# Token-row loads of q, k and V by GpSimd from the fourth batch on, in a kernel of windowed attention and a two-layer MLP

## The chip, the core and the metric

The kernel runs on one core of a Trainium2 chip. Its engines are TensorE (PE; the profile shows its weight loads apart, as PEld), VectorE (DVE), ScalarE (ACT), GpSimd (POOL) and SyncE (SP); 16 DMA engines move data between memory and the core. The metric is the time of one execution in microseconds, the median over several runs.

## The reference

Eight batches of eight heads, 576 tokens, head dimension 64. Every token attends to itself and the 63 before it; the attention output, as 4608 rows of 512, goes through two matrix products with `h - tanh(h)` between them.

```python
scores = scale * np.matmul(q, k.transpose(0, 1, 3, 2))
mask = (rel >= 0) & (rel < window)          # window = 64
attn = softmax(np.where(mask, scores, -1e9))
x = np.matmul(attn, v).transpose(0, 2, 1, 3).reshape(4608, 512)
h = x @ w_in                                 # 512 x 2048
out = (h - np.tanh(h)) @ w_out               # 2048 x 512
```

Inputs and output are float32. The kernel computes in bfloat16 with float32 sums.

## The kernel before

**The MLP sets the beat.** Rows are cut into nine chunks of 512 tokens. A chunk has 16 steps: `hp_mm` (four matmuls of 512 columns, L304) makes one 128-row slice of h in a PSUM bank that alternates between two, ScalarE takes the tanh (L308), VectorE subtracts (`g_sub`, L314) into `gT`. Sixteen steps later `yp_mm` (four matmuls, L324) uses those slices for the output, ScalarE copies a finished tile (`y_out`, L329) and SyncE stores it. The program is a list of half-steps h: at even h stands `hp_mm` of step h/2, at odd h `yp_mm` of step h/2 - 16. Everything else is hung on a half-step by `at(h, function, ...)` and is issued there, after the MLP's matmul and before the subtraction. There is no scheduler: each engine does its instructions in just that order, and waits where data is not there.

**Attention works on pairs of heads.** A batch b has four pairs; pair pr takes heads pr and pr + 4, and g = 4b + pr counts pairs. For a pair, q and k are needed transposed (`qT`, `kT`: 128 rows are two heads of 64 columns); `scores` (L247) multiplies a span of 128 keys with 64 queries of both heads, nine times, and ScalarE takes the exponential; `masking` (L255) clears what is outside the window; `pv` (L261) multiplies with V and a column of ones; `norm` (L268, L272) divides. `x_dma` (L293) transposes the batch's result by DMA into the MLP's `xT`.

**V as key spans.** `vw` (two buffers, by the parity of the batch) holds for each of nine spans j its 128 keys as partitions: keys 64j to 64j+63 in partitions 64 to 127, the 64 keys before them in partitions 0 to 63, and per head 64 columns and a one.

**How batches 3 to 7 get their data.** The first three batches follow a script of steps (`PLAN`), which is the same in both kernels. From the fourth batch (b = 3) a loop places the work. With s = 32b - (0, 2, 4, 4, 4) and a = 8g - 48 - (the same), so that a = s - 48 for a batch's first pair and 8 more for each next one:

- V: one GpSimd DMA with cast to bfloat16 (`load_v_all`, L151, 72 partitions of 8 tokens) at s-78; a GpSimd copy per pair into `vb` (`cast_v`, s-72 on); nine SyncE DMAs that lay `vb` out as spans (`keys_v`, L161, from s-54), one that copies the upper halves into the lower (`shift_v`, L169, s-47).
- q and k: one GpSimd DMA each with cast (`load_all`, L101, 96 partitions of 6 tokens, so 1,536 contiguous bytes a row and head), k at s-64 and q at s-60. For b below 7: a GpSimd copy per pair into rows of two heads (`cast`, a-7 and a-5), six TensorE transposes of 96 rows (`tr`, L234, q at a, k at a+2), and the eviction of PSUM (ScalarE and VectorE for q, ScalarE for k), with a stride of six tokens.
- For b = 7, GpSimd copies instead into a zero-padded `qz` (`cast_q`, L120) and into rows of k; SyncE writes both to DRAM (`bounce`, L126 and L130) and reads them back transposed (`tr_dma`, L137 and L140).
- `pace` (L108) is a GpSimd copy of one element that waits for the subtraction of step h/2 - 1, so that a load does not start earlier.

For all of them, scores stand at a+5, a+7 and a+9, masking at a+11, `pv` at a+13 to a+15, `norm` at a+15.

Of the kernel before, what the change touches and what calls it, by code (L numbers as in the profile page):

```python
# [8 lines left out]
BF16 = mybir.dt.bfloat16  # L9
# [6 lines left out]
def kernel(  # L16
# [9 lines left out]
    nc = tc.nc  # L26
    B, H, S, D = q.shape
    NP = H // 2
    NJ = S // 64
    E, P = 6, S // 6  # L30
    EV, PV = 8, S // 8
    d_model = moe_w_in.shape[0]
    d_ff = moe_w_in.shape[1]
    NT = B * S
# [8 lines left out]
    const = ctx.enter_context(tc.tile_pool(name="const", bufs=1))  # L43
    qk_pool = ctx.enter_context(tc.tile_pool(name="qk", bufs=3))
    all_pool = ctx.enter_context(tc.tile_pool(name="all", bufs=2))
# [2 lines left out]
    sm_pool = ctx.enter_context(tc.tile_pool(name="sm", bufs=3))  # L48
    xt_pool = ctx.enter_context(tc.tile_pool(name="xt", bufs=3))
    g_pool = ctx.enter_context(tc.tile_pool(name="g", bufs=2))  # L50
    dram = ctx.enter_context(tc.tile_pool(name="dram", bufs=2, space=bass.MemoryType.DRAM))
    psum = ctx.enter_context(tc.tile_pool(name="psum", bufs=1, space=PSUM))


# [1 line left out]
    ps = psum.tile([128, 8, 512], F32, name="ps")  # L56

    ident = const.tile([128, 128], BF16, name="ident")
# [7 lines left out]
    NR, NPT = 2, 4  # L66
# [3 lines left out]
    vw = [const.tile([128, NJ, H, D + 1], BF16, name=f"vw{i}") for i in range(2)]  # L70
    vb = const.tile([PV, EV, H, D + 1], BF16, name="vb")
    PT = [const.tile([128, NJ, 128], BF16, name=f"pt{i}") for i in range(NPT)]
    kT = [const.tile([128, 64 + S], BF16, name=f"kt{i}") for i in range(NR)]
    qT = [const.tile([128, 2, S], BF16, name=f"qt{i}") for i in range(NR)]
    qz = [const.tile([P, 2, E, 128], BF16, name=f"qz{i}") for i in range(2)]
    xs = [const.tile([128, NJ, NP, D], BF16, name=f"xs{i}") for i in range(2)]

    stage, rows, whole = {}, {}, {}

    def move(eng, o, i):  # L80
        if eng is nc.scalar:
            nc.scalar.activation(o, i, ACT.Copy)  # L82
        else:
            eng.tensor_copy(o, i)  # L84

    def load(g, n, eng):

        b, pr = divmod(g, NP)
        if eng is nc.gpsimd:
            if (b, n) not in whole:  # L90
                whole[b, n] = all_pool.tile([P, H, E * D], BF16, tag=n, name=n + "all")
            t = whole[b, n][:, pr::NP]
        else:
            t = qk_pool.tile([P, 2, E * D], F32, tag="f", name=n + "f")
        eng.dma_start(out=t, in_=(q if n == "q" else k)[b, pr::NP].rearrange("h (p e) d -> p h (e d)", e=E))
        stage[g, n] = t

    def load_all(b, n):

        t = all_pool.tile([P, H, E * D], BF16, tag=n, name=n + "all")  # L100
        nc.gpsimd.dma_start(out=t, in_=(q if n == "q" else k)[b].rearrange("h (p e) d -> p h (e d)", e=E))  # L101
        for pr in range(NP):
            stage[b * NP + pr, n] = t[:, pr::NP]
# [6 lines left out]
    def cast(g, n, eng=nc.gpsimd):  # L110
# [1 line left out]
        move(eng, t.rearrange("p e h d -> p h e d"),  # L112
             stage.pop((g, n)).rearrange("p h (e d) -> p h e d", d=D))
        rows[g, n] = t

    def cast_q(g):

        i = stage.pop((g, "q")).rearrange("p h (e d) -> p h e d", d=D)
        for h in range(2):
            nc.gpsimd.tensor_copy(qz[g % 2][:, h, :, 64 * h:64 * h + 64], i[:, h])  # L120

    def bounce(g, n):

        if n == "q":
            t = dram.tile([2, S, 128], BF16, tag="q", name="qd")
            nc.sync.dma_start(out=t.rearrange("h (p e) c -> p h (e c)", e=E),  # L126
                              in_=qz[g % 2].rearrange("p h e c -> p h (e c)"))
        else:
            t = dram.tile([S, 128], BF16, tag="k", name="kd")
            nc.sync.dma_start(out=t.rearrange("(p e) c -> p (e c)", e=E),  # L130
                              in_=rows.pop((g, "k")).rearrange("p e h d -> p (e h d)"))
        rows[g, n + "d"] = t

    def tr_dma(g, n):
        t = rows.pop((g, n + "d"))
        if n == "q":
            nc.sync.dma_start(out=qT[g % NR].rearrange("c h s -> c (h s)"),  # L137
                              in_=t.rearrange("h s c -> (h s) c"), transpose=True)
        else:
            nc.sync.dma_start(out=kT[g % NR][:, 64:], in_=t, transpose=True)  # L140

    def load_v(b, pr):
        if (b, "v") not in whole:
# [20 lines left out]
    def shift_v(b, j0, j1, eng=nc.sync):  # L164
        lo, hi = vw[b % 2][0:64, j0 + 1:j1 + 1], vw[b % 2][64:128, j0:j1]
        if eng is nc.vector:
            eng.tensor_copy(lo, hi)
        else:
            eng.dma_start(out=lo.rearrange("p j h c -> p (j h c)"), in_=hi.rearrange("p j h c -> p (j h c)"))  # L169

    w_in_r = moe_w_in.rearrange("(ko ki) f -> ki ko f", ki=128)

# [23 lines left out]
    def more_constants():  # L196
# [7 lines left out]
        for h in range(2):  # L204
# [2 lines left out]
                                    base=-1, pattern=[[-1, 64]], channel_multiplier=1)  # L207
            nc.gpsimd.affine_select(hide[:, h], hide[:, h], compare_op=ALU.is_ge, fill=-(2.0 ** 30),
                                    base=64, pattern=[[1, 64]], channel_multiplier=-1)

    def more_zeros(i):
        nc.gpsimd.memset(qz[i], 0.0)

    def make_mask():
        nc.gpsimd.memset(seen, 1.0)
# [41 lines left out]
    def pv(g, grp):  # L257
        b, pr = divmod(g, NP)
        for i in range(3):
            j = 3 * grp + i  # L260
            nc.tensor.matmul(ps[:, 5 + grp, 130 * i:130 * i + 130], PT[g % NPT][:, j, :],  # L261
                             vw[b % 2][:, j, 2 * pr:2 * pr + 2, :], start=True, stop=True)

    def norm(g):
        b, pr = divmod(g, NP)
# [71 lines left out]
    def at(h, *fn):  # L337
        items.setdefault(h, []).append(fn)
# [14 lines left out]
    def play(script):  # L353
        for step in script.split():
            what = step[0]
            n = [int(i, 36) for i in step[1:] if i not in "apvs"]
            eng = [ENG[i] for i in step[1:] if i in "apvs"]
            if what in "qr":
                load(*n, "q" if what == "q" else "k", *eng)
            elif what in "QK":  # L360
                load_all(*n, what.lower())
# [12 lines left out]
            elif what == "z":  # L374
                for j in (0, 4) if eng[0] is nc.vector else (0,):
                    shift_v(*n, j, j + 4 if eng[0] is nc.vector else NJ - 1, *eng)
            elif what == "E":
                tr(*n, "q", 3, *eng)
            elif what == "F":
                tr(*n, "k", 2 if n[0] < 2 * NP else 3, *eng)  # L380
            elif what == "R":
                scores(*n, (4, 0, 1)[n[1]] if n[0] < NP else 4)
            elif what == "P":
                for i in range(3):
                    pv(*n, i)
                norm(*n)
            elif what == "M":
                masking(*n)
            elif what == "X":
                b, half, part = n  # L390
                x_tr(b, half, 4 * part, 4 + 5 * part, 2 if part == 1 and b < 2 else 3, *eng)
            elif what == "Y":
                x_dma(*n)
            elif what == "w":
                load_w_in(*n)
            elif what == "o":
                load_w_out(*n)
            elif what == "i":
                make_ident()
            elif what == "n":  # L400
                make_mask()
            elif what == "m":
                more_constants()
# [27 lines left out]
    for h, script in PLAN.items():  # L431
        at(h, play, script)

    for i in range(2):
        at(66 + 2 * i, more_zeros, i)


    for g in range(3 * NP, B * NP):
        b, pr = divmod(g, NP)
        a = 8 * g - 48 - (0, 2, 4)[min(b - 3, 2)]  # L440
        s = 32 * b - (0, 2, 4)[min(b - 3, 2)]
        at(s - 72 + 5 * pr, cast_v, b, pr)
        if b < 7:
            at(a - 7, cast, g, "q")
            at(a, tr, g, "q", 3, nc.scalar, nc.vector)
        else:
            at(a - 14, cast_q, g)
            at(a - 12, bounce, g, "q")
            at(a - 6, tr_dma, g, "q")
        if b < 7:  # L450
            at(a - 5, cast, g, "k")
            at(a + 2, tr, g, "k", 3, nc.scalar)
        else:
            at(a - 13, cast, g, "k")
            at(a - 11, bounce, g, "k")
            at(a - 5, tr_dma, g, "k")
        for i in range(3):
            at(a + 5 + 2 * i, scores, g, i, 4)
        at(a + 11, masking, g)
        for i in range(3):  # L460
            at(a + 13 + i, pv, g, i)
        at(a + 15, norm, g)
        if pr == NP - 1:
            at(a + 16, x_dma, b)
        for j in range(NJ):
            if pr == 0:
                at(s - 54 + j // 2, keys_v, b, j)
        if pr == 0:
            if b < 4:
                at(s - 78, load_v_all, b)  # L470
                at(s - 64, load_all, b, "q")
                at(s - 63, load_all, b, "k")
            else:
                hq, hk = s - (60 if b < 7 else 68), s - (64 if b < 7 else 72)
                for h, f in (s - 78, (load_v_all, b)), (hq, (load_all, b, "q")), (hk, (load_all, b, "k")):
                    at(h, pace, h)
                    at(h, *f)
            at(s - 47, shift_v, b, 0, NJ - 1)

    LAG = 16  # L480
    for h in range(min(items), 2 * (16 * NC + LAG) + 2):
        n = h // 2
        c, m = divmod(n, M)
# [41 lines left out]
```

## Time and profile before

Three runs took 353.01, 354.48 and 355.05 us, a median of 354.48. The profiled execution's span, from its first to its last instruction, is 351.4 us.

| Group (line, engine) | instructions | busy us | mean of one, ns |
|---|---|---|---|
| L304 PE, h | 576 | 147.7 | 380 |
| L324 PE, out | 576 | 146.1 | 381 |
| L247 PE, scores | 288 | 36.4 | 226 |
| L261 PE, PV | 288 | 29.6 | 226 |
| L234 PE, transposes of q and of k | 168 + 168 | 12.6 + 12.2 | 214, 210 |
| L314 DVE, subtraction | 144 | 99.3 | 691 |
| L272 DVE, norm | 64 | 48.3 | 755 |
| L308 ACT, tanh | 144 | 85.9 | 597 |
| L84 POOL, copies of V, k, q | 29 + 26 + 24 | 30.6 + 21.7 + 20.0 | 1069, 837, 832 |
| L167 DVE, lower half of `vw`, in the first batches | 4 | 3.3 | 854 |

How to read it: an instruction's duration is from its start to its end, and matmuls overlap, so four L304 matmuls of 380 ns advance the chain by 0.86 us. A group's line gives busy time and mean, then the idle time of its engine just before it and what ended most of it. The chain of waits follows what ended last back through the execution; each piece is start, length, engine or DMA, what it writes, line. The slices cut the span in 40 equal parts (8.8 us each) and give the busy share in tenths. In the DMA view a packet's size is what it writes; a queue's share is the time that its packets took as a share of 16 engines' time, and goes over 100% where packets of one engine overlap.

### The profile page before, as it was taken

What the parts mean: (1) busy time and instruction counts of PE and PEld (TensorE: products, weight loads), DVE (VectorE), ACT (ScalarE), POOL (GpSimd) and SP (SyncE); (2) the same over time, 40 slices, a digit from 0 to 9 for tenths busy, and PEclk for the clock granted to TensorE, in tenths of its full rate; (3) what the DMA queues carried; (4) which work ended last, traced back from release to release, by engine and by line L of the source; (5) the groups of instructions that cost most, each with busy time, mean ns of one, the idle gap of its engine ahead of it and who ended that gap; (6) DMA issues with size and microseconds to landing.
All of it is one profiled execution on the core that took longest, in us unless ns stands there. A gap on an engine that the chain in (4) does not pass through costs nothing.

```text
span 351.4 us, 5740 instructions
## 1 busy us (share of the span) xinstructions
PE 315.1 (90%) x2173; PEld 179.0 (51%) x2173; DVE 199.0 (57%) x314; ACT 192.8 (55%) x347; POOL 112.0 (32%) x160
## 2 busy tenths in 40 slices
PE   0267788899899999999999999997999999999995
PEld 0256366555555555555555555553555444444442
DVE  1336786867676666666776766663656333344400
ACT  1467479765556665666566666652554444444411
POOL 7829543833338325422642264410000000000000
PEclk9988999999999999999999999998999999999999
DMA  8699999969777696958494895669711400010021
GB/s 175 126 164 190 175 189 173 183 133 180 161 148 112 127 137 146 139 126 156 102 160 105 164 169 123 130 147 206 189 46 38 121 32 30 31 60 30 30 89 62
DMA packets 54436, 43.98 MB, mean 125 GB/s; under 512 B 25144, under 2 KB 48248, under 8 KB 54024
## 3 DMA queue, kind: packets, MB, share of 16 engines
q0 software_dynamic: 20512, 18.22, 35.8%
q1 hardware_dynamic: 33128, 24.37, 27.0%
q10 hardware_dynamic: 768, 1.02, 1.0%
q8 instruction: 17, 0.28, 0.3%
q14 instruction: 11, 0.09, 0.1%
HBM read 36.70 MB, written 11.21 MB: 136 GB/s over the span
## 4 chain that ended last, share of the span: by engine, by line
PE 78%; DVE 7%; DMA 5%; ACT 5%; POOL 2%; issue 2%; SPq 0%; ACTq 0%; DVEq 0%; POOLq 0%
PE ps L324 34%; PE ps L304 32%; PE ps L261 5%; PE ps L247 4%; DVE xs L272 3%; PE ps L234 3%; DMA vw<-vb 3%; DMA vall<-in_v_dram 2%; DVE gT L314 2%; ACT th L308 1%; DVE qt L84 1%; ACT pt L251 1%; ACT qt L82 1%; DMA kt<-kd 1%; DVE pt L255 1%
## 5 line engine op out<-in xcount | busy, mean ns | idle before, releaser
L314 DVE TENSOR_TENSOR gT<-ps,th 128x512 bf16<-128x512 f32 x144 | 99.3, 691 | 94.9 <-ACT th L308 92.6
L304 PE MATMUL ps<-xT,wi 128*128 128x512 bf16 x576 | 147.7, 380 | 1.7 <-DVE gT L314 1.7
L324 PE MATMUL ps<-w_out_sb,gT 128*128 128x512 bf16 x576 | 146.1, 381 | 0.2 <-ACT ysb L329 0.2
L308 ACT ACTIVATE th<-ps 128x512 f32<-128x512 f32 x144 | 85.9, 597 | 79.8 <-PE ps L304 79.5
L304 PEld LDWEIGHTS <-wi 128*128 128x128 bf16 x576 | 61.4, 114 | 47.7 <-issue 3.6
L324 PEld LDWEIGHTS <-gT 128*128 128x128 bf16 x576 | 54.3, 98 | 55.9 <-issue 1.0
L251 ACT ACTIVATE pt<-ps 128x384 bf16<-128x384 f32 x96 | 46.9, 490 | 44.9 <-PE ps L247 38.3
L272 DVE TENSOR_TENSOR xs<-ps,rc 64x576 bf16<-64x576 f32 x64 | 48.3, 755 | 1.5
L84 POOL COPY vb<-vall 72x1024 bf16<-72x1024 bf16 x29 | 30.6, 1069 | 52.8 <-DMA vall<-in_v_dram 40.2
L247 PE MATMUL ps<-qt,kt 128*128 128x128 bf16 x288 | 36.4, 226 | 8.5 <-ACT pt L251 3.8
L261 PEld LDWEIGHTS <-pt 128*128 128x128 bf16 x288 | 22.7, 101 | 19.8 <-issue 3.6
L261 PE MATMUL ps<-vw,pt 128*128 128x130 bf16 x288 | 29.6, 226 | 3.4 <-DVE xs L272 1.1
L247 PEld LDWEIGHTS <-kt 128*128 128x128 bf16 x288 | 24.4, 102 | 12.1 <-DMA kt<-kd 2.1
L329 ACT ACTIVATE ysb<-ps 128x512 f32<-128x512 f32 x36 | 21.5, 597 | 16.0 <-PE ps L324 16.0
L84 DVE COPY qt<-ps 64x576 bf16<-64x576 bf16 x24 | 18.2, 759 | 18.1 <-ACT qt L82 18.1
L84 POOL COPY kb<-kall 96x768 bf16<-96x768 bf16 x26 | 21.7, 837 | 13.0 <-DMA kall<-in_k_dram 12.1
L84 POOL COPY qb<-qall 96x768 bf16<-96x768 bf16 x24 | 20.0, 832 | 16.8 <-DMA qall<-in_q_dram 16.8
L82 ACT ACTIVATE qt<-ps 64x576 bf16<-64x576 bf16 x32 | 20.3, 636 | 1.0 <-PE ps L234 0.6
L82 ACT ACTIVATE kt<-ps 128x576 bf16<-128x576 bf16 x25 | 16.2, 648 | 4.3 <-PE ps L234 4.0
L255 DVE TENSOR_TENSOR pt<-pt,ps 128x1152 bf16<-128x1152 bf16 x24 | 17.9, 745 | 0.0
L234 PE MATMUL ps<-ident,kb 96*128 96x96 bf16 x168 | 12.2, 210 | 2.7 <-ACT xT L82 0.9
L234 PEld LDWEIGHTS <-kb 96*128 96x128 bf16 x168 | 10.2, 100 | 7.4 <-issue 2.7
(52 smaller groups left out, 123.4 us busy)
## 6 DMA issues: line engine op xcount, KB each, us to landing
out_dram<-ysb SPq DMA_DIRECT2D x36, 256.0 KB
vall<-in_v_dram POOLq DMA_DIRECT2D x7, 576.0 KB, 10.0
kall<-in_k_dram POOLq DMA_DIRECT2D x7, 576.0 KB, 8.8
qall<-in_q_dram POOLq DMA_DIRECT2D x7, 576.0 KB, 8.8
vw<-vb SPq DMA_DIRECT2D x61, 65.0 KB
vw<-vw SPq DMA_DIRECT2D x6, 520.0 KB
w_out_sb<-in_moe_w_out_dram POOLq DMA_DIRECT2D x4, 512.0 KB, 8.4
qd<-qz SPq DMA_DIRECT2D x4, 288.0 KB
```

The lines of the kernel that those rows point to most:

```text
L82: nc.scalar.activation(o, i, ACT.Copy)
L84: eng.tensor_copy(o, i)
L234: nc.tensor.transpose(tp[:, e, :], src[:, e, :], ident[:P, :P])
L247: nc.tensor.matmul(sp[:, i, :], kT[g % NR][:, 64 * j:64 * j + 128], qT[g % NR][:, :, 64 * j:64 * j + 64], start=True, stop=g >= 2 * NP)
L251: nc.scalar.activation(PT[g % NPT][:, 3 * grp:3 * grp + 3, :], sp, ACT.Exp, scale=scale)
L261: nc.tensor.matmul(ps[:, 5 + grp, 130 * i:130 * i + 130], PT[g % NPT][:, j, :], vw[b % 2][:, j, 2 * pr:2 * pr + 2, :], start=True, stop=True)
L272: nc.vector.tensor_tensor(xo[r, :, :, pr, :], ov[r, :, :, h, 0:D], rc[r].to_broadcast([64, 3, 3, 64]), ALU.mult)
L304: nc.tensor.matmul(hp, w_in_tile(ki, m), chunk_tile(c)[:, :, ki % 2, 64 * (ki // 2):64 * (ki // 2) + 64], start=(ki == 0), stop=(ki == 3))
L308: nc.scalar.activation(th, hp, ACT.Tanh)
L314: nc.vector.tensor_tensor(gT[c][:, m, :], hp, th, ALU.subtract)
L324: nc.tensor.matmul(yp, gT[c][:, m, s * 128:(s + 1) * 128], w_out_sb[:, m, :], start=(m == 0), stop=(m == M - 1))
L329: nc.scalar.activation(ysb, ps[:, yp_bank(c, s), :], ACT.Copy)
```

## The change

For batches 3 to 7 all loads become token rows: a partition is a token, a row is one head's 64 values (256 bytes read, 128 written).

- V: five GpSimd DMAs (`load_rows`, half-steps s-59 to s-55) put blocks of 128 tokens straight into `vw`: block i fills both halves of span 2i+1, the last one (64 tokens) the upper half of span 8. Heads stand in their own order, so `pv` takes columns of heads pr and pr + 4 by a stride. At s-42, `cross_rows` has VectorE copy the remaining halves, two copies of 64 partitions by 2,080.
- q and k: five blocks of 128 tokens (the last of 64), for each block two GpSimd DMAs (heads 0 to 3 and 4 to 7), from s-68 for q and s-63 for k, each after a `pace`. `tr_tokens` transposes a block's two heads straight out of the loaded tile: four transposes of 128 rows and one of 64 in place of six of 96, for all five batches.
- The GpSimd copies, the span and shift DMAs, and batch 7's way through DRAM are gone.

```diff
+    NF = S // 128
-    qz = [const.tile([P, 2, E, 128], BF16, name=f"qz{i}") for i in range(2)]
...
+    def load_rows(b, i):
+        w, n = vw[b % 2], min(128, S - 128 * i)
+        nc.gpsimd.dma_start(out=w[:, 2 * i + 1, :, 0:D] if i < NF else w[64:128, 2 * i, :, 0:D],
+                            in_=v[b, :, 128 * i:128 * i + n].rearrange("h p d -> p h d"))
+    def cross_rows(b):
+        w = vw[b % 2]
+        nc.vector.tensor_copy(w[0:64, 2::2], w[64:128, 1::2])
+        nc.vector.tensor_copy(w[64:128, 0:NJ - 1:2], w[0:64, 1::2])
+    def load_tokens(b, n, i):
+        if i == 0:
+            t = all_pool.tile([128, H, E * D], BF16, tag=n, name=n + "all")
+            t = t.rearrange("p h f -> p (h f)")[:, 0:(NF + 1) * H * D]
+            whole[b, n] = t.rearrange("p (i r h d) -> p i r h d", r=NP, h=2, d=D)
+        c = min(128, S - 128 * i)
+        src = (q if n == "q" else k)[b, :, 128 * i:128 * i + c].rearrange("(h r) p d -> p h r d", h=2)
+        for h in range(2):
+            nc.gpsimd.dma_start(out=whole[b, n][0:c, i, :, h, :], in_=src[:, h])
+    def tr_tokens(g, which, bank, *engs):
+        b, pr = divmod(g, NP)
+        tp = ps[:, bank, :].bitcast(BF16)[:, 0:S]
+        for i in range(NF + 1):
+            c = min(128, S - 128 * i)
+            nc.tensor.transpose(tp[:, 128 * i:128 * i + c],
+                                whole[b, which][0:c, i, pr].rearrange("p h d -> p (h d)"), ident[:c, :c])
+        if which == "q":
+            move(engs[0], qT[g % NR][0:64, 0], tp[0:64])
+            move(engs[1], qT[g % NR][64:128, 1], tp[64:128])
+        else:
+            move(engs[0], kT[g % NR][:, 64:], tp)
...
-                             vw[b % 2][:, j, 2 * pr:2 * pr + 2, :], start=True, stop=True)
+                             vw[b % 2][:, j, pr::NP, :] if b > 2 else vw[b % 2][:, j, 2 * pr:2 * pr + 2, :], start=True, stop=True)
...
-        at(s - 72 + 5 * pr, cast_v, b, pr)
-        if b < 7:
-            at(a - 7, cast, g, "q")
-            at(a, tr, g, "q", 3, nc.scalar, nc.vector)
-        else:
-            at(a - 14, cast_q, g)
-            at(a - 12, bounce, g, "q")
-            at(a - 6, tr_dma, g, "q")
...
+        at(a, tr_tokens, g, "q", 3, nc.scalar, nc.vector)
+        at(a + 2, tr_tokens, g, "k", 3, nc.scalar)
...
         if pr == 0:
+            for i in range(NF + 1):
+                at(s - 59 + i, load_rows, b, i)
+            at(s - 42, cross_rows, b)
+        if pr == 0:
+            for n, h in ("q", s - 68), ("k", s - 63):
+                at(h, pace, h)
+                for i in range(NF + 1):
+                    at(h + i, load_tokens, b, n, i)
```

More of the change, by code (lines that the diff above doesn't have):

```diff
@@ L50 @@
     g_pool = ctx.enter_context(tc.tile_pool(name="g", bufs=2))
-    dram = ctx.enter_context(tc.tile_pool(name="dram", bufs=2, space=bass.MemoryType.DRAM))
     psum = ctx.enter_context(tc.tile_pool(name="psum", bufs=1, space=PSUM))
@@ L90, in load @@
             if (b, n) not in whole:
-                whole[b, n] = all_pool.tile([P, H, E * D], BF16, tag=n, name=n + "all")
+                whole[b, n] = all_pool.tile([128, H, E * D], BF16, tag=n, name=n + "all")[0:P]
             t = whole[b, n][:, pr::NP]
@@ L98, in load_all @@
     def load_all(b, n):
-        t = all_pool.tile([P, H, E * D], BF16, tag=n, name=n + "all")
+        t = all_pool.tile([128, H, E * D], BF16, tag=n, name=n + "all")[0:P]
         nc.gpsimd.dma_start(out=t, in_=(q if n == "q" else k)[b].rearrange("h (p e) d -> p h (e d)", e=E))
@@ L114, in cast @@
         rows[g, n] = t
[L116 to L127, printed above, removed]
-        else:
[L129 to L140, printed above, removed]
     def load_v(b, pr):
@@ L209, in more_constants @@
                                     base=64, pattern=[[1, 64]], channel_multiplier=-1)
-    def more_zeros(i):
-        nc.gpsimd.memset(qz[i], 0.0)
     def make_mask():
@@ L432 @@
         at(h, play, script)
-    for i in range(2):
-        at(66 + 2 * i, more_zeros, i)
     for g in range(3 * NP, B * NP):
@@ L441 @@
         s = 32 * b - (0, 2, 4)[min(b - 3, 2)]
-        at(s - 72 + 5 * pr, cast_v, b, pr)
-        if b < 7:
-            at(a - 7, cast, g, "q")
-            at(a, tr, g, "q", 3, nc.scalar, nc.vector)
-        else:
-            at(a - 14, cast_q, g)
-            at(a - 12, bounce, g, "q")
-            at(a - 6, tr_dma, g, "q")
[L450 to L456, printed above, removed]
+        at(a, tr_tokens, g, "q", 3, nc.scalar, nc.vector)
+        at(a + 2, tr_tokens, g, "k", 3, nc.scalar)
         for i in range(3):
@@ L464 @@
             at(a + 16, x_dma, b)
-        for j in range(NJ):
-            if pr == 0:
-                at(s - 54 + j // 2, keys_v, b, j)
         if pr == 0:
[L469 to L478, printed above, removed]
+            for i in range(NF + 1):
[6 more added lines that the diff above has]
+                    at(h + i, load_tokens, b, n, i)
     LAG = 16
```

## The prediction

> **What bounds the kernel.** I read the page's busy shares and slices first, then the chain of waits, then windows by stage, then the DMA view.
>
> ```profile
> PE 315.1 (90%) x2173; PEld 179.0 (51%) x2173; DVE 199.0 (57%) x314; ACT 192.8 (55%) x347; POOL 112.0 (32%) x160
> ...
> PE   0267788899899999999999999997999999999995
> ...
> POOL 7829543833338325422642264410000000000000
> ...
> DMA  8699999969777696958494895669711400010021
> ```
>
> TensorE is full from about 70 us to the end, with one dent: the slice 237 to 246 us shows 7. GpSimd has room. The DMA engines are 60 to 90% busy while batches 3 to 7 are loaded. The chain of waits around the dent, and two windows (time, then busy us of PE, PEld, DVE, ACT, POOL, granted clock, DMA share, GB/s):
>
> ```profile
> 235.68 0.88 PE ps L304 x4
> 236.56 0.99 SPq L137
> ...
> 237.59 2.65 DMA kt<-kd
> ...
> 241.76 1.71 PE ps L324 x4
> ...
> 246.26 0.17 PE ps L247 x3
> ```
> ```profile
> 217.70:236.60 18.90, 18.90 (x122) 10.29 (x120) 12.69 (x20) 11.19 (x22) 7.38 (x12) 1.00 0.59 134
> 236.60:240.30 3.70, 1.15 (x8) 0.50 (x6) 0.93 (x2) 0.58 (x1) 0.00 (x0) 1.00 0.86 174
> 240.30:244.80 4.50, 4.50 (x23) 2.42 (x24) 1.63 (x3) 1.58 (x3) 0.00 (x0) 0.63 0.94 232
> ```
>
> Batch 7's k goes through DRAM and a DMA transpose, and TensorE waits for it from 236.56 to 240.29: 3.7 us. Then the granted clock is half for 3.4 us (241.4 to 244.8; four L324 matmuls need 1.71 us instead of 0.86), which costs another 1.7. The dent is 5.4 us. Elsewhere after 70 us TensorE is the limit: a group of 8 half-steps holds 8 x 0.86 us of large matmuls, 9 + 9 small ones at 0.17 us per three and 12 transposes at 0.26 us per six ("PE ps L234 x6" in the chain), 8.4 us; the steps of L304 do advance 1.06 us per half-step between 144 and 211 us. So in this stretch only TensorE work and lateness count.
>
> **Part 1, batch 7 leaves the DMA transposes.** Gone: the dent, -5.4. Added: 4 pairs x 2 groups of transposes on TensorE. A new group is four 128-column transposes and one of 64; at the 0.057 us of a 128-column L247 matmul (0.17 for three) that is 4 x 0.057 + about 0.04 = 0.27, so 8 x 0.27 = +2.1. Its evictions (per pair 0.64 + 0.65 us on ACT, 0.76 on DVE) hide in ACT and DVE idle time: ACT works 11.2 and DVE 12.7 of 18.9 us there. Bounds: if part of the dent was slack the steps would regain anyway, the gain is the 3.7 alone; the elapsed time checks it: 36.2 us for half-steps 172 to 204 by the starts of L304 against 32 x 1.054 = 33.7 dense, a gain of 2.5. Net -2.5 to -3.3; I take -3.3, since it comes from the dent itself.
>
> **Part 2, transposes of batches 3 to 6.** Five of 128 columns replace six of 96: 0.27 against 0.26 us a group, 32 groups: +0.3 at most, 0 taken. The evictions write dense columns instead of a stride of 6: nothing I can price; ACT and DVE are not the bound. L261's right operand becomes two runs of 65 four heads apart: same 130 columns; 0 taken, and a strided row would show there.
>
> **Part 3, casts leave GpSimd, 9 span DMAs and a shift leave SP.** Per batch some 8 x 0.83 + 4 x 1.07 = 10.9 us of GpSimd copies and 10 SP issues of 0.5 to 0.6 us go. Neither queue ends the chain there: 0, except that DMA work falls, counted below.
>
> **Part 4, two DVE copies per batch** (64x2080 bf16; L167 has four of this shape, 698 ns median, 1.32 the longest): 1.4 us at half-step s-42. DVE waits 1.0 to 1.5 us per step for the tanh (L314 idle before: 94.9 us over 144), so most is covered; behind the copies stands the L314 subtraction of the same step, which frees the bank that L304 needs two steps on. For batch 3 (step at 95.3 us) DVE idles 1.19 us before the 97.04 subtraction and masking waits behind it: 0.2 us leaks. I take 0.2 per batch, +1.0 in all; bounds 0 and 5 x 1.4 = 7.
>
> **Part 5, 25 loads of 256-byte rows instead of 3 large ones.** This decides. Each batch needs 3 x 576 x 8 = 13,824 packets of 256 B read and 128 B written, where q and k had 768 packets of 768 B each.
>
> ```profile
> L151 POOL DMA_DIRECT2D vall<-in_v_dram x7 | 6.0, 855 | 1.1 <-POOL tick L108 1.1
> L101 POOL DMA_DIRECT2D qall<-in_q_dram x7 | 5.5, 788 | 1.7 <-issue 1.7
> ...
> L176 POOL DMA_DIRECT2D wi<-in_moe_w_in_dram x3 | 2.3, 778 | 0.0
> ...
> L95 POOL DMA_DIRECT2D qall<-in_q_dram x2 | 1.3, 648 | 0.0
> ```
>
> Issue on GpSimd: a q or k block is 512 rows, as a w_in load is (778 ns); the last block is 256 rows, between 648 (192 rows) and 778: 0.70; a V block of 1,024 rows is put at V's own 0.86 (0.99 if the step from 648 to 778 is continued). 16 x 0.778 + 4 x 0.70 + 4 x 0.86 + 0.78 = 19.5 us a batch, of the 34 that a batch lasts. The four V loads of L146 go out back to back into interleaved columns, so such writes are not made to wait for one another. An issue of 768 rows ends in 0.78 us and the copy behind it keeps its 1.04 us, so no row costs GpSimd more than 1.0 ns: bounds 16 (25 x 0.65) and 25 us. All hide while a batch's issues take under about 24 us: behind them on GpSimd stand only the pace copies (L108, a wait for the L314 subtraction of a step long past) and more loads. Batch 3 starts latest, since casts of batch 2 hold GpSimd until 69.6 us: k's issues end at 85 us and V's at 89, due at 89.1 (half-step 50) and 95.3, so a landing of over 4 us there is late.
>
> Transfer: windows of one kind of packet alone.
>
> ```profile
> q0 software_dynamic: 509, 0.39, 127.7%
> ```
> ```profile
> q1 hardware_dynamic: 822, 0.21, 111.6%
> ```
>
> The first is 148 to 150 us, k or q with the cast: 509 packets of 768 B in 2 us, 16 x 2000 / 509 = 62.9 ns of an engine each. The second is 139 to 140 us, transposes of 256 B without cast: 19.5 ns each. A new packet lies between: 19.5 and 62.9. Single cast packets of the trace last 79 ns (768 B written), 98 (1024), 173 (2048) and 324 (4096): 22 + 0.074 per byte, so 31.5 at 128 B; in the plateau packets overlap, 62.9 against 79, a factor 0.8. 0.8 x 31.5 = 25 ns, which I take: 13,824 x 25 / 16 = 21.6 us a batch; bounds 16.8 and 54.3.
>
> The Trainium skill speaks against this: DMA: Bandwidth & Descriptors, Specifications, asks for at least 512 B, below which an engine reads, modifies and writes. The 256-byte packets at 19.5 ns here show no such doubling. If it doubled a cast packet, 63 ns, the loads would take 54 us a batch and the kernel would be slower by about 150 us, my upper bound in any case.
>
> When are they due? q's issue starts at s-68, and the last V must be there at s-42: 26 half-steps, 27.7 us at 1.064 (batch 3: 67.9 to 95.3 us, 27.4). V lands at 1.5 (issue to first packet, 105.85 to 107.3 us for k) + 0.9 (the longest first packets) + 21.6 + 2.2 (stores: 720 packets cost 74.7 ns each between 300 and 330 us, 4 x 144 of them a batch, 26/32 of it) = 26.2 us. That is 1.5 us early, and the DVE copy can slip 2.1 us more before L304's bank is late (two steps of 2.13, less 1.4 for the copies and 0.75 for the subtraction). The point from which it decides is 25 + 3.6 x 16 / 13.824 = 29 ns a packet. q (7.6 us of issues for 21) and k (15.2 for 23 from the same start) have more room. Price taken: 0.
>
> **Sum.** -5.4 + 2.1 + 1.0 = -2.3 on a span of 351.4: 349.1. The median of the runs, 354.48, is 3.1 above the span; the same distance gives 352.2.
>
> **Rivals.**
> (A) The above, loads on time: 352.2, own range 350.3 to 354.5 (copies at 0 give 351.2, one us below that for waits of batch 3's removed casts; above, a gain of 2.5 and 2 us more of leak).
> (B) V is late in every batch, the new wait being the DVE copy for V's load, with L314 and the masking queued behind it. At 31.5 ns without overlap V lands after 31.8 us: 4.1 late, 2.1 of it slack, 2.0 us of stall, and a stop of that length costs 1.7 of half clock as the dent did: 3.7 x 5 = 18.5, 371 us. For it: 29 ns is only 4 above my value, the rows are scattered over four heads and V's rows start on odd 130-byte steps. Against it: 13,824 packets would fill 27 of 34 us, and stores and x transposes need only 5.5. At the upper bound of 62.9: 54.3 + 4.6 - 27.7 - 2.1 = 29.1 + 1.7, times 5 = 154, 506 us.
> (C) Loads on time, but the DVE copies lie on the path whole, 7 us: 354.5 - 3.3 + 7 = 358. Against it the DVE idle time in every step.
> (D) The dent's place is taken by another wait of batch 7 (V's spans held TensorE 0.63 us at 238 too), and little is gained: 354 to 355.
>
> **Chances.** A 0.50, B 0.32 near 371 and 0.06 far above, C 0.05, D 0.07. The 0.5% that a measurement of this kernel can tell is 1.8 us: under 352.7 or over 356.3. A falls two thirds below 352.7 (0.34, with a little of D 0.36), the rest and D within (0.17), B and C slower (0.47). The likeliest is A, 352.2; the range reaches up to 372 to take in B as priced, and leaves out its tail and the far end.
>
> **What would show it.** Right: no gap at L304 near 237 us and a clock of 1.00 there; GpSimd with 25 issues per batch of 0.65 to 0.9 us and no copies after 70 us but ticks; packets of 128 B under 29 ns each; the two DVE copies preceded by no DMA wait. Wrong: DVE waiting for V's load by microseconds in each batch, DMA at 9 throughout 70 to 240 us, half clock in stretches (B); L314 late after the copies (C); issues of 1.2 us and more, 30 us a batch, would make GpSimd's queue the bound and also end in B's place.

## The result, and the profile after

The changed kernel took 358.02 us (median of 4 runs, 357.82 to 360.62) against 354.70 for the kernel before beside it: a ratio of 1.0153, 95% interval 1.0107 to 1.0198. Measured again on another occasion it was 1.0133 (1.0088 to 1.0179). It is slower by about 5 us, where 2.3 us less was forecast. (The ratios in this document are taken over fast runs alone; the plain medians differ by 3.3 us here and by 4.4 the second time.) The profiled span is 356.1 us.

The page of the changed kernel, first its busy shares and slices, then the group lines of the parts that are new (line numbers have moved: L310 is h, L330 is out, L172 the new transposes, L165 and L147 the loads of q, k and V, L153 and L154 the two VectorE copies):

```profile
PE 322.6 (91%) x2151; PEld 185.6 (52%) x2181; DVE 203.3 (57%) x328; ACT 197.2 (55%) x355; POOL 137.2 (39%) x202
...
PE   0369788899899999999999999999999999999995
...
POOL 7829444789229805950496059500000000000000
...
DMA  8799999999939926990699099904000410010012
```
```profile
L165 POOL DMA_DIRECT2D qall<-in_q_dram x50 | 36.0, 765 | 1.6 <-issue 1.2 <-PE ps L172 0.3
...
L172 PE MATMUL ps<-ident,qall 128*128 128x128 bf16 x80 | 7.7, 219 | 0.0
...
L172 PE MATMUL ps<-ident,qall 64*128 64x64 bf16 x20 | 4.0, 200 | 0.0
...
L153 DVE COPY vw<-vw 64x2080 bf16<-64x2080 bf16 x5 | 3.5, 697 | 0.2
L154 DVE COPY vw<-vw 64x2080 bf16<-64x2080 bf16 x5 | 3.5, 696 | 0.1
```

What was feared is not there. The dent is gone and TensorE is full from 100 us to the end. The 25 loads of a batch are issued in 18.6 us (137.5 to 156.1 for batch 5), and nothing waits for them: the VectorE copies stand 0.1 and 0.2 us idle in all. TensorE is as busy as before, only for longer. So the chain of waits has to be read piece by piece, at the same place of a batch in both kernels. Each piece is start, length, engine, what it writes, line. The kernel before:

```profile
173.44 0.86 PE ps L304 x4
174.31 0.26 PE ps L234 x6
174.56 0.86 PE ps L324 x4
175.43 0.17 PE ps L247 x3
175.60 0.86 PE ps L304 x4
```

The changed kernel:

```profile
203.42 0.86 PE ps L310 x4
204.28 0.35 PE ps L172 x5
204.63 0.97 PE ps L330 x4
205.60 0.17 PE ps L253 x3
205.77 0.86 PE ps L310 x4
206.63 0.36 PE ps L172 x5
206.99 0.16 issue
207.15 0.81 PE ps L330 x3
```

Five transposes take 0.35 us where six took 0.26, and the out matmuls behind them take 0.97 us instead of 0.86; in the second group the same loss shows as 0.16 us of "issue" (one of the four matmul records is missing there). A group therefore costs 0.46 us, not 0.27. In the trace's single records the four 128-row transposes start 0.055 us apart, as matmuls of 128 columns do. The weight load of the 64-row one starts 0.147 us after the fourth, and the weight load behind it another 0.133 us later. In all 40 groups it is the same within 0.003 us, but for one in batch 3 that entered 0.025 us sooner. In the kernels below whose transposes all have 128 or all have 96 rows, the loads start 0.06 and 0.04 us apart.

The table splits the profiled executions by the starts of the h matmuls; the half-steps before 16 are left out, since the start took 55 to 59 us, differently from execution to execution.

| Kernel | half-steps 128 to 160, us | 176 to 192, us | 16 to the end, us |
|---|---|---|---|
| before, the profile of the prediction | 33.8 | 20.4 | 295.6 |
| before, three more executions | 33.8, 33.8, 33.8 | 17.6, 17.3, 17.9 | 293.4, 292.6, 293.2 |
| after, twice | 35.4, 35.4 | 17.7, 17.7 | 299.2, 299.2 |
| after, last block of 128 rows | 34.0 | 17.0 | 293.3 |
| after, six blocks of 96 rows | 33.9 | 16.9 | 293.1 |
| after, without the VectorE copies | 35.4 | 17.7 | 298.9 |
| before, batch 7 on TensorE | 33.8 | 16.9 | 293.2 |
| before, a 64-row transpose added | 35.6 | 16.7 | 297.9 |
| before, a 96-row transpose added | 34.1 | 17.5 | 293.9 |
| before, two 64-row transposes added | 35.9 | 16.8 | 299.8 |
| last block of 128 rows, loads 8 half-steps later | 39.9 | 17.8 | 318.7 |

Half-steps 128 to 160 hold eight groups of transposes and no stall in either kernel: 1.6 us more, 0.20 a group. From 16 to the end the change costs 6.2 us against the three later executions of the kernel before.

### The profile page after: what moved, and what is told of

Read it like the earlier page. It is cut to its first block, busy times and chain, and to the rows that moved or that the text cites. A ratio compares the mean times of both kernels' runs of the same rounds, so it can differ in the third digit from the quotient of the medians.

```text
span 356.1 us, 5749 instructions
## 1 busy us (share of the span) xinstructions
PE 322.6 (91%) x2151; PEld 185.6 (52%) x2181; DVE 203.3 (57%) x328; ACT 197.2 (55%) x355; POOL 137.2 (39%) x202
## 4 chain that ended last, share of the span: by engine, by line
PE 83%; ACT 5%; DVE 4%; DMA 4%; issue 3%; POOL 1%; ACTq 0%; DVEq 0%; POOLq 0%
PE ps L330 35%; PE ps L310 33%; PE ps L267 5%; PE ps L253 4%; PE ps L172 4%; DMA vw<-vb 2%; DMA vall<-in_v_dram 2%; ACT pt L257 1%; DVE xs L278 1%; ACT th L314 1%; PE ps L240 1%; PE ps L256 1%; DVE qt L83 1%; DVE gT L320 1%; ACT qt L81 1%
## 5 line engine op out<-in xcount | busy, mean ns | idle before, releaser
L310 PE MATMUL ps<-xT,wi 128*128 128x512 bf16 x576 | 147.3, 379 | 1.8 <-DVE gT L320 1.7
L330 PE MATMUL ps<-w_out_sb,gT 128*128 128x512 bf16 x546 | 139.8, 380 | 3.3 <-issue 2.5
L310 PEld LDWEIGHTS <-wi 128*128 128x128 bf16 x576 | 60.9, 113 | 47.5 <-issue 3.1
L330 PEld LDWEIGHTS <-gT 128*128 128x128 bf16 x576 | 52.2, 97 | 55.3 <-issue 0.5
L165 POOL DMA_DIRECT2D kall<-in_k_dram x50 | 36.4, 761 | 1.7 <-DMA qall<-in_q_dram 1.4
L165 POOL DMA_DIRECT2D qall<-in_q_dram x50 | 36.0, 765 | 1.6 <-issue 1.2
L107 POOL COPY tick<-gT 1x1 bf16<-1x1 bf16 x10 | 1.8, 177 | 61.1 <-DVE gT L320 47.3
L83 DVE COPY qt<-ps 64x576 bf16<-64x576 bf16 x28 | 15.2, 544 | 17.5 <-ACT qt L81 17.5
L81 ACT ACTIVATE qt<-ps 64x576 bf16<-64x576 bf16 x36 | 22.9, 636 | 1.5 <-PE ps L172 0.9
L147 POOL DMA_DIRECT2D vw<-in_v_dram x25 | 21.9, 937 | 0.0
L81 ACT ACTIVATE kt<-ps 128x576 bf16<-128x576 bf16 x29 | 18.8, 648 | 4.2 <-PE ps L240 4.0
L261 DVE TENSOR_TENSOR pt<-pt,ps 128x1152 bf16<-128x1152 bf16 x24 | 17.9, 744 | 0.0
L83 POOL COPY vb<-vall 72x1024 bf16<-72x1024 bf16 x9 | 9.5, 1082 | 11.8 <-DMA vw<-vb 7.0
```

Of the source, the lines that this page charges most:

```text
L147: nc.gpsimd.dma_start(out=w[:, 2 * i + 1, :, 0:D] if i < NF else w[64:128, 2 * i, :, 0:D], in_=v[b, :, 128 * i:128 * i + n].rearrange("h p ...
L165: nc.gpsimd.dma_start(out=whole[b, n][0:c, i, :, h, :], in_=src[:, h])
L310: nc.tensor.matmul(hp, w_in_tile(ki, m), chunk_tile(c)[:, :, ki % 2, 64 * (ki // 2):64 * (ki // 2) + 64], start=(ki == 0), stop=(ki == 3))
L330: nc.tensor.matmul(yp, gT[c][:, m, s * 128:(s + 1) * 128], w_out_sb[:, m, :], start=(m == 0), stop=(m == M - 1))
```

## The experiments

The theory "row height" is that the one 64-row transpose per group stops TensorE; the height is the number of partitions that the transposed block takes. Its rivals are "source" (transposes straight out of the loaded tile are slow as such) and "loads" (data is late).

### The last block of 128 rows

```diff
-        c = min(128, S - 128 * i)
-        src = (q if n == "q" else k)[b, :, 128 * i:128 * i + c].rearrange("(h r) p d -> p h r d", h=2)
+        t0 = min(128 * i, S - 128)
+        src = (q if n == "q" else k)[b, :, t0:t0 + 128].rearrange("(h r) p d -> p h r d", h=2)
...
-            nc.tensor.transpose(tp[:, 128 * i:128 * i + c],
-                                whole[b, which][0:c, i, pr].rearrange("p h d -> p (h d)"), ident[:c, :c])
+            nc.tensor.transpose(tp[:, t0:t0 + 128],
+                                whole[b, which][:, i, pr].rearrange("p h d -> p (h d)"), ident)
```

> The changed kernel, but the last block of q and of k holds the last 128 tokens (448 to 575) instead of the last 64, so all five transposes of a group have 128 rows; 64 columns of PSUM are written twice with the same values, and q and k move 5% more packets. Theory 'row height': the 64-row transpose among 128-row matmuls costs about 0.19 us a group, since the weight load before it and the one behind it wait for the array (group 0.46 us instead of 5 x 0.055 = 0.275): 40 groups x 0.185 = -7.4, so 350.6 us. Rival 'source': transposes out of the loaded tile are slow as such (a strided, DMA-written weight operand, waits for ten loads each): the group stays at 0.46 and the time at 358. Rival 'loads': the loss is late data, 358 or a little more with the extra packets.

Measured: 352.12 us, 1.0012 of the kernel before (0.9975 to 1.0050). (q and k move 11% more packets, not 5.) Its chain:

```profile
203.46 0.28 PE ps L172 x5
203.74 0.86 PE ps L330 x4
```

Still five transposes, out of the same tile, behind the same loads, and the group is 0.28 us with nothing added to the out matmuls behind it. 5.9 us from 16 to the end are gone: "row height" stands, "source" and "loads" fall. It is less than the 7.4 expected: from half-step 128 on, the 18 groups gave 0.18 us each, but the 22 before it 2.6 us together instead of 4.1. Of these, 14 gave 0.18 too, six 0.1 and two (half-steps 50 and 58) nothing, and at half-steps 90 and 120 the kernel with 128 rows takes 0.2 and 0.3 us longer: so much of the loss had been slack.

### Six blocks of 96 rows

```diff
+    NB = S // 96
...
-        c = min(128, S - 128 * i)
-        src = (q if n == "q" else k)[b, :, 128 * i:128 * i + c].rearrange("(h r) p d -> p h r d", h=2)
+        c = 96
+        src = (q if n == "q" else k)[b, :, 96 * i:96 * i + c].rearrange("(h r) p d -> p h r d", h=2)
```

> The changed kernel with q and k loaded in six blocks of 96 tokens (12 DMAs of 384 rows each instead of 10): six 96-row transposes a group, no 64-row one, same packets. 'Row height': group 6 x 0.043 = 0.26 us as before the change, 358.0 - 40 x 0.20 = 350 us. 'Source': six slow transposes instead of five, 358 to 361. GpSimd issues 4 more DMAs of 0.7 us a batch, 3 us of some 13 free.

Measured: 351.49 us, 0.9981 (0.9947 to 1.0015). Without a 64-row transpose, and with the same packets as the change, the loss is gone again; a group is 0.26 us as before the change (here L173 are the transposes, L331 is out):

```profile
203.02 0.26 PE ps L173 x6
203.28 0.86 PE ps L331 x4
```

Its median is the lowest of the versions of the change, but its interval overlaps that of the last block of 128 rows, and it cannot be told from the kernel before.

### One more transpose, of 64 or 96 rows, in the kernel before

```diff
+        if g >= 3 * NP:
+            spare = ps[:, bank, :].bitcast(BF16)
+            for x in range(1):
+                nc.tensor.transpose(spare[:, 640 + 64 * x:640 + 64 * x + 64], src[0:64, 0, :], ident[:64, :64])
```

The second kernel has 96 in place of 64 throughout, the third `range(2)`.

> The kernel before with one more transpose at the end of each of the 32 groups of batches 3 to 6: 64 rows, into columns of PSUM that nobody reads. 'Row height': 0.19 for the switch of row height and 0.03 to 0.05 for the transpose, 32 x 0.23 = +7.4, 362 us. Rivals 'source' and 'loads' (a 64-row transpose is a small matmul like others, 0.04): +1.3, 356.

> The same with 96 rows in the added transpose: all theories, 32 x 0.043 = +1.4, 356.1 us. If this one too costs 7 us, the added instruction counts and not its height.

> The same with two 64-row transposes one behind the other. If the switch into and out of 64 rows costs, the second adds only its 0.03 to 0.05: 32 x 0.27 = +8.6, 363 us. If each 64-row instruction costs 0.2, +14, 369 us.

Measured: 357.23 us, 1.0110 (1.0049 to 1.0172) with one of 64 rows; 353.72, 1.0016 (0.9970 to 1.0062) with one of 96; 357.87, 1.0142 (1.0080 to 1.0204) with two of 64. The medians hold less than expected, as some groups had slack and batch 7's waits came out shorter in these executions; half-steps 128 to 160 settle it: 1.8 us for eight added 64-row transposes, 0.23 each as expected; 0.3 us for 96 rows, 0.04 each; 2.1 us for pairs of 64, 0.26 a pair. The chain, first with one (L234 are the six of 96 rows, L238 the added one, L328 the out matmuls), then with two:

```profile
143.70 0.26 PE ps L234 x6
143.96 0.13 PE ps L238
144.09 0.97 PE ps L328 x4
```
```profile
170.00 0.26 PE ps L234 x6
170.26 0.16 PE ps L238 x2
170.42 0.97 PE ps L328 x4
```

The second adds 0.03 us. A 64-row transpose is also only 64 columns wide; that its width is not the cause shows in the weight loads of the kernel with two of them:

```profile
170.01 0.10 PEld L234 LDWEIGHTS <-qb 96*128 96x128 bf16 x1
170.19 0.11 PEld L238 LDWEIGHTS <-qb 64*128 64x128 bf16 x2
170.35 0.11 PEld L328 LDWEIGHTS <-gT 128*128 128x128 bf16 x2
```

The first 64-row load starts 0.18 us after the last 96-row one, and the 128-row load 0.15 us after the second 64-row one; between the two of 64 rows, behind a transpose just as narrow, it is 0.015 us. It is the step into 64 rows and out of it that costs, not the instruction, and it costs the same in a kernel that has nothing of the change.

The Trainium skill has a rule that fits: TensorEngine Tiling (Array Packing), Tiling Modes, says that changing the tiling mode drains TensorE, and its list of modes has 64-row tiles beside the full 128 rows. The trace agrees as far as it goes: 96 rows between 128 cost nothing extra, 64 rows cost 0.2 us in and out. That a plain 64-row transpose counts as such a mode is a reading; no run here shows it by itself.

### Batch 7 on TensorE, nothing else

```diff
-        if b < 7:
+        if b < 8:
             at(a - 7, cast, g, "q")
             at(a, tr, g, "q", 3, nc.scalar, nc.vector)
...
-                hq, hk = s - (60 if b < 7 else 68), s - (64 if b < 7 else 72)
+                hq, hk = s - 60, s - 64
```

> The kernel before with one part of the change alone: batch 7 also goes through the GpSimd casts and TensorE's six 96-row transposes, its loads at the half-steps of the batches before it. Part 1 of the prediction (dent of 5.4 us gone, 8 groups of 0.26 us added): -3.3, 351.4 us. Rival: the dent's place is taken by another wait, 354 to 355.

Measured: 352.27 us, 1.0024 (0.9983 to 1.0065), so none of the 3.3 us. The wait for `kt<-kd` is gone from its trace and half-steps 176 to 192 take 16.9 us, as foreseen; what the kernel before loses there is smaller than its profile had shown. So it was profiled three times more:

> The kernel before, profiled again, to see how large the dent of batch 7 is from execution to execution (half-steps 176 to 192 by the starts of the h matmuls; 20.4 us in the first profile, about 15.8 without a wait). Theory 'steady dent': 20 to 21 us again, 5.4 us to be gained. Theory 'chance dent' (the two kernels with added transposes in batches 3 to 6 alone, whose batch 7 is untouched, showed 16.6 and 17.5): 16 to 18 us, so 1 to 2 us to be gained, which the 2.1 us of added transposes take back.

> The same again, a second execution: 'steady dent' 20 to 21 us for half-steps 176 to 192, 'chance dent' 16 to 18.

> The same again, a third execution: 'steady dent' 20 to 21 us for half-steps 176 to 192, 'chance dent' 16 to 18.

17.6, 17.3 and 17.9 us, never 20.4. The second of these executions, TensorE's timeline (start, us, engine, line, what it does, and in brackets the idle time before it) and the chain at the same place:

```profile
236.27 1.03 PE L324 MATMUL ps<-w_out_sb,gT 128*128 128x512 bf16 x4
237.13 0.38 PE L261 MATMUL ps<-vw,pt 128*128 128x130 bf16 x3
238.71 0.34 PE L247 MATMUL ps<-qt,kt 128*128 128x128 bf16 x3 [1.20 <-DMA kt<-kd]
```
```profile
235.63 3.04 DMA kt<-kd
238.66 0.05 issue
238.71 0.34 PE ps L247 x3
239.05 0.86 PE ps L304 x4
```

The chain gives 3.04 us to the DMA, but TensorE worked on beside it and was idle for 1.20 only. The same reading of the first profile:

```profile
238.09 0.27 PE L261 MATMUL ps<-vw,pt 128*128 128x130 bf16 x2 [0.63 <-DMA vw<-vw]
240.29 0.34 PE L247 MATMUL ps<-qt,kt 128*128 128x128 bf16 x3 [1.92 <-DMA kt<-kd]
```

TensorE was idle for 2.55 us there (0.63 for V's spans and 1.92 for k), where the prediction read 3.7 off the chain, and 1.7 us of half clock came on top. In each of the three later executions the wait for k is 1.2 us, with 0 to 0.6 us more for V's spans, and the granted clock stays at full: the L304 matmuls behind take 0.86 us at once. Over half-steps 160 to 208 the three executions took 49.9, 49.5 and 50.1 us, and batch 7 on TensorE takes 50.2.

### Without the two VectorE copies

```diff
-            at(s - 42, cross_rows, b)
```

> The changed kernel without the two VectorE copies per batch: half of the key spans of batches 3 to 7 keep old data (this part of V is left out). The prediction's 0.2 us of leak per batch: 357.0. If the copies lay on the path whole (rival C, 1.4 x 5): 351. If they are covered: 358.0.

Measured: 356.84 us, 1.0165 (1.0105 to 1.0224), which is no less than the 1.0153 and 1.0133 of the whole change. From 16 to the end 0.3 us are gone, all of it in half-steps 48 to 64, where batch 3 has its copies. In the other four batches the copies are covered.

### Loads 8 half-steps later

```diff
-                at(s - 59 + i, load_rows, b, i)
+                at(s - 51 + i, load_rows, b, i)
...
-            for n, h in ("q", s - 68), ("k", s - 63):
+            for n, h in ("q", s - 60), ("k", s - 55):
```

on the kernel with the last block of 128 rows.

> The kernel with the last block of 128 rows, and all loads of batches 3 to 7 placed 8 half-steps later (q s-60, k s-55, V s-51). Rival B's mechanism: V's last packets came 20 us (18 to 19 half-steps) after the first issue in the changed kernel, now at about s-41 against s-42, and k at s-46 against s-46: on the edge, so 0 to 2 us a batch, 351 to 361 us. If the loads had no room before (B as the cause of the loss), 8 half-steps of 1.06 us in each of five batches: 351 + 40 = 390.

Measured: 375.39 us, 1.0594 (1.0509 to 1.0678), more than the 0 to 2 us a batch that I expected, less than the 40 of a kernel without room. k, not V, is late: its waits, and one stretch after such a wait (time, busy us of PE, PEld, DVE, ACT, POOL, granted clock, DMA share, GB/s):

```profile
PEld L172 <- DMA kall<-in_k_dram: 14.5, 7, 3.6
PE ps L172 <- DMA kall<-in_k_dram: 14.3, 9, 3.4
```
```profile
136.00:142.30 6.30, 5.97 (x20) 2.64 (x21) 1.24 (x2) 1.74 (x3) 0.35 (x1) 0.50 0.92 60
```

14.3 us of waiting, and four stretches of half clock of 3.4 to 6.8 us (20.5 us together, half of it lost) make up some 24.5 of the 25.4 us by which 16 to the end grew. (The profiled execution is the longest of the four, 379.97 us; the medians are 23.3 us apart.) So late loads, which rival B feared for V, are dear when they come; in the change as it stands TensorE waits for none of the new loads.

### The change once more

> The changed kernel again, timed beside the kernel before on this chip: the ratio 1.0153 of its first measurement should come back within 0.5%. In its profile half-steps 48 to 208 take the same 6 us more than in the kernel with the last block of 128 rows (row height), and half-steps 176 to 192 take 17.7 us again, since no DMA stands there in TensorE's way.

357.96 us, 1.0133 (1.0088 to 1.0179), and the three columns of the table came back to a tenth. Its first profile was no accident.

## Why the prediction was wrong, point by point

- **Part 2, the step that failed.** "four 128-column transposes and one of 64; at the 0.057 us of a 128-column L247 matmul ... 0.27" priced the 64-row transpose by its columns, from rows of full height. It costs 0.46 us a group, 0.18 to 0.20 more than the same group without 64 rows; 40 groups, and 6 us from 16 to the end after slack. The 0 taken for batches 3 to 6 and the 2.1 for batch 7 both rest on it, and none of the rivals had this loss. The trace of before held one 64-row transpose (L220, at the start): its weight load starts at 13.81 us and the next one at 13.97, 0.16 us apart, where the 96-row loads behind it are up to 0.08 apart (0.04 later, in the full stretch). One such row would have been a hint and no price, but it was the nearest, and I did not look for it.
- **Part 1, a term of the wrong size.** The dent was counted with 5.4 us. "TensorE waits for it from 236.56 to 240.29: 3.7 us" took a piece of the chain, which is a DMA's time, for TensorE's idle time: the window shown beside it had 1.15 us of matmuls in it, so 2.55. And in the three later executions it is 1.2 to 1.8 us, without the half clock. Against the 2.1 us of added work the part is worth nothing, not -3.3; the elapsed time that I used as a check came from the same execution and could not find this.
- **Part 3, right.** GpSimd and SP lose work, and no gain shows: with 128 or 96 rows the change takes as long as the kernel before.
- **Part 4, right in sign.** The copies take 0.70 us each as priced. They cost 0.3 us in batch 3 (0.2 forecast) and nothing in the others, where 0.2 each was taken.
- **Part 5, right in the main.** A packet of 128 bytes lasts 32 ns in the records (31.5 forecast), and 13,824 of them go through in 20.1 us for batch 4, 23.3 ns an engine each (25 taken). 25 issues take 18.6 us (19.5 forecast); a V load of 1,024 rows takes 0.97 us, where 0.86 was taken and 0.99 named. From q's first issue to V's last packet it is 21.9 us for batch 4 (26.2 forecast): the packets are there at 126.4 us and the copy starts at 132.6. The doubled packet of 63 ns that the prediction weighed did not show.
- **The sum.** With the measured sizes, +6.0 for the row height, +0.3 for batch 7 on TensorE and 0 for the rest make 6.3; the profiles show 6.2. ("0 for the rest" is a balance: against batch 7 on TensorE, the kernel with 128 rows takes 0.4 us more in half-steps 48 to 64, 0.1 more in most of the others, and 0.9 less in 80 to 96, 112 to 128 and at the end together.) The time lies in the stated range by luck: the range reached up to 372 for the late loads of rival B, which did not come. That rival C was priced at 358 is chance too: without its copies the loss stays. The chances beside it were not added up rightly: B, its far end and C make 0.43, not 0.47, and the middle is 0.21, not 0.17.

## What to carry to other kernels

When TensorE is the bound, price its small matmuls by their shapes in rows as well as columns, and look for a row of the same height in the trace. A remainder block of 64 rows can be dearer than a full one that repeats half of its neighbour. A DMA's piece in the chain of waits is no engine's idle time, and a stall that one profile shows may belong to that execution alone: read the engine's own timeline, in two or three executions, before a stall's removal is counted as a gain.

## What was not expected of the hardware

- A step from 128 or 96 rows to 64 and back costs TensorE 0.18 to 0.20 us; a second 64-row transpose behind the first adds 0.03.
- TensorE's waits of 1.2 us (three executions) and of 1.5 us (the kernel with the 96-row transpose) left its clock at full; waits of 0.63 and 1.92 us close together were followed by 3.4 us of half clock, those for late loads (up to 3.4 us at once) by 3.4 to 6.8 us.
- VectorE's eviction of q from dense columns of PSUM took 0.46 us in the changed batches; where it takes the tokens in turn from six blocks of 96 columns, it took 0.76. In the kernel before this eviction stands on the chain in places (at 132.87 us, for one), so the shorter one may be why the kernel with 128 rows is 0.3 us quicker in half-steps 80 to 96 and 112 to 128. The prediction gave it no price, and no run tested it alone.
